# Loads and transposes at the head of the last stage: wo by one transfer a chunk, a gated tile loaded before the products end, and a gated tile's transposes moved behind the attention products

## The chip, the cores and the metric

The kernel runs on one core of one Trainium2 chip. The metric is the device time of one execution in microseconds (us), as the median of several runs. Beside it the hardware profiler recorded one execution, whose rows are shown below. TensorE is written PE (matmuls, transposes) and PEld (its weight loads), VectorE is DVE, ScalarE is ACT, GpSimd is POOL, and SP is SyncE, which issues most of the transfers; SPq is SP's queue of issues.

## The reference

x is 2048 tokens by 512, all in float32. The result is x plus two mixers of the layer-normed x:

```python
xn = layernorm(x)
# A: 32 heads of 16, feature map phi(t) = [softmax(t @ w_phi), softmax(-t @ w_phi)] per head
num = phi(q) @ (phi(k)^T @ v);  den = phi(q) . sum(phi(k)) + 1e-6
A = (num / den) @ wo                              # wo 512 x 512
# B: gated MLP with a product over the tokens
z1, z2 = halves of gelu(xn @ w_in)                # 688 columns each
g = w_sp @ layernorm(z2) + b_sp                   # w_sp 2048 x 2048
B = (z1 * g) @ w_out                              # w_out 688 x 512
out = x + A + B
```

## The kernel before

Tokens go in 16 tiles of 128. Every large product is made of three TensorE passes over operands that are split in a high and a low part (`mm3`, lines L51, L52, L53; the high part is rounded by ACT at L43, `round_h`, and the low part is the rest, made by DVE at L47, `rest_l`). The stages follow each other: projections of q, k, v with the features, the two halves of the gated MLP's input, the product with w_sp (seven products of half the size in both directions, in 32 steps; the loop's steps are numbered n, NC is their count), and a last stage. What each stage needs later goes through arrays in device memory: `e_d` holds the exponentials of the q features, `u_d` the gated tiles, `kvT_d` the summed phi(k)^T v.

The last stage takes token tiles in pairs. For tiles i and i+1 a round consists of:

- `attend_T`: 16 TensorE transposes of the features into `ptq` (L749 where the tile is plain float32, L751 otherwise), and four ACT copies into `f` (L753);
- `attend`: 32 small products `po` of `f` and `kvT` (L765), then two ACT and two DVE instructions that split the result into `oT`;
- `gated`/`gate_T` for each tile: four transposes into `ptu` (L640), two more in a second `ptu` (L644, L645), then ACT and DVE split them into `uh`, `ul` and `rt` (L43, L47, L648);
- `project_u` for each tile: 17 matmuls into `pout` by the split w_out (`wu`; 15 of `mm3` and two at L779);
- `project_o` for each tile: 12 matmuls into the same `pout`, by the split wo (`wo_h`, `wo_l`, named `woh` and `wol` in the profile), then a DVE add of x (L788) and the store (L789).

The gated tile `u` for token tile i comes by `load_u` (L634) from `u_d`. Tile 0 is loaded and transposed during the products (`first_gate`, its tile is named `u_uh`); tile 1 is loaded by `fetch_u`, whose memory, a pool called `cw`, takes the space that the products' operands leave. `slot()` gives buffers of another pool, 16 wide, freed earlier. wo is loaded in four chunks of 128 rows: `load_w` takes for every chunk four pieces of 32 rows, each piece 64 rows from the next in wo, and lays them under each other in a tile `wof`; then `round_h` and `rest_l` split it.

The order of instructions on each engine is set by a tile scheduler, which places an instruction by its own estimate; `tc.issue_after(x)` only holds the scheduler from placing an instruction ahead of x. `lasts` keeps the last instruction of some steps for that: `lasts[2]` the last transpose of a gated tile, `lasts[3]` the last `po` product. SP issues its transfers in its own order, and the eight completion semaphores of SP's queue go round: an issue waits until the transfer eight places earlier on SP has landed.

Of the kernel before, what the change touches and what calls it, by code (L numbers as in the profile page):

```python
# [10 lines left out]
F32 = mybir.dt.float32  # L11
F32R = mybir.dt.float32r
# [6 lines left out]
P = 128  # L19
S, D, H, DH, FH = 2048, 512, 32, 16, 688  # L20
# [3 lines left out]
NG = 4  # L24
NF = 2 * D
KF = FH // P
REM = FH - KF * P
# [4 lines left out]
HP, QP = P // 2, P // 4  # L32
# [3 lines left out]
def mixer(ctx: ExitStack, tc: tile.TileContext, x, x_t, wv, wqkT, phi_bd, wo, w_in, wst, b_r, w_out, out):  # L36
    nc = tc.nc
    pe, act, dve, pool, sp = nc.tensor, nc.scalar, nc.vector, nc.gpsimd, nc.sync


    def round_h(eng, h, src):
        if eng is act:
            return act.activation(h, src, AF.Copy).ins  # L43
        return eng.tensor_copy(h, src).ins

    def rest_l(l, src, h, eng=None):
        return (eng or dve).tensor_tensor(l, src, h.bitcast(F32), op=ALU.subtract).ins  # L47
# [113 lines left out]
    with ExitStack() as p0:  # L161
# [32 lines left out]
        def fold(wT, g, accs):  # L194
            gs = slice(g * P, (g + 1) * P)
            for c, acc in accs:
                ins = pe.matmul(acc[:, gs], wT[g][:, c * P:(c + 1) * P], bd[:, gs], start=g == 0, stop=g == NG - 1,
                                skip_group_check=True).ins
            return ins
# [26 lines left out]
        def split_x(src):  # L226
            t = xz.tile([P, 2, FH], F32R, tag="xz", name="xT")
            xT.append(t)
            src = src.rearrange("p a b -> p (a b)")
            return round_h(act, t[:, 0, :D], src), rest_l(t[:, 1, :D], src, t[:, 0, :D])  # L230

        def stats(s):
            st6 = wk.tile([P, 6], F32, tag="st6", name="st6")
            dve.bn_stats(st6, xt[s])
            nm = wk.tile([P, 1], F32, tag="nm", name="nm")
            ins = dve.bn_aggr(mv_x[:, s], st6).ins
            pool.tensor_scalar_mul(nm, mv_x[:, s, 0:1], -1.0)
            rstd_of(mv_x[:, s], r_x[:, s:s + 1])
            return nm, ins
# [4 lines left out]
        def transposed(s):  # L244
            xs = xt.pop(s)
            pt = ps.tile([P, ND, P], F32, tag="mm", name="pt")
            for c in range(ND):
                ins = pe.transpose(pt[:, c], xs[:, c * P:(c + 1) * P], ident).ins  # L248
            return pt, ins
# [46 lines left out]
        with ExitStack() as queue:  # L296
# [3 lines left out]
            nm, i = stats(0)  # L300
            keep(dve=i, act=center(0, nm))
            accs = [(c, (za, kv_ps_p)[c // 2].tile([P, D], F32, tag="z", name="fold")) for c in range(ND)]
            for g in range(NG):
                if g == NG - 1:
                    pt, i = transposed(0)
                    keep(pe=i)
                keep(pe=fold(wkT, g, accs))
            i, j = split_x(pt)
            keep(act=i, dve=j)
            nm, i = stats(1)  # L310
# [10 lines left out]
            pt, i = transposed(1)  # L321
            keep(pe=i)
            i, j = split_x(pt)
            keep(act=i, dve=j)
            nm, i = stats(2)
# [3 lines left out]
            for k in range(2):  # L329
                accs = [(2 * k + m, za.tile([P, D], F32, tag="z", name="fold")) for m in range(2)]  # L330
                for g in range(NG):
                    i = fold(wqT, g, accs)
                folded(0, accs)
                if k == 0:
                    keep(pe=i)
                    pt, i = transposed(2)
# [63 lines left out]
    def load_a(n):  # L400
        i, q = SEQ[n]
        f = []
        for k in range(2):
            t = ws.tile([P, QC, P], F32, tag=f"f{k}", bufs=2, name="wf")
            sp.dma_start(t, wst[2 * i + k, :, q * QC:(q + 1) * QC, :])
            f.append(t.rearrange("p (k two) t -> p two k t", two=2))
        return f
# [128 lines left out]
    for s in range(NT):  # L536
# [13 lines left out]
        r = zw.tile([P, 1], F32, tag="rstd", bufs=2, name="rstd")  # L550
# [24 lines left out]
    def load_z1(i):  # L575
        t = gt.tile([P, 2, FH + REM], F32, tag="z1", name="z1t")
        for k in range(2):
            pool.dma_start(t[:, k, :FH], z1_d[2 * i + k])
        return t

    def products(n, g):
        i, q = SEQ[n]
        ops = A.pop(n)
        for name, an, bn in FORM:
            if n % NQ == 0:
                g[name] = psg.tile([P, D], F32, tag="g", name="g")
            dst = g[name][:, :FC]
            for k in range(2):
                (ah, al), (bh, bl) = ops[an], B[2 * q + k][bn]
                mm3(dst, (ah[:, k], al[:, k]), (bh, bl), n % NQ == 0 and k == 0, n % NQ == NQ - 1 and k == 1)  # L590
# [16 lines left out]
    def gate(i, cb, z):  # L607
        cb, first, _ = cb
        with tc.issue_after(first):
            act.activation(z[:, :, :FH], z[:, :, :FH], AF.Gelu_apprx_tanh)  # L610
        zs = z[:, :, :FH].rearrange("p k (j f) -> p k j f", j=2)
        dve.tensor_tensor(zs, zs, cb.rearrange("p (k j) f -> p k j f", k=2), op=ALU.mult)
        rm = slice(KF * P, FH)
        rh = gt.tile([P, 2, REM], F32R, tag="rh", name="rh")
        dve.tensor_copy(rh, z[:, :, rm])
        rest_l(z[:, :, FH:FH + REM], z[:, :, rm], rh)
        dve.tensor_copy(z[:, :, rm], rh.bitcast(F32))
        for k in range(2):
            pool.dma_start(u_d[2 * i + k], z[:, k])
# [3 lines left out]
    def slot(name, dt=F32):  # L623
        return xz.tile([P, 2, FH], dt, tag="xz", name=name).rearrange("p a b -> p (a b)")

    def load_w(src, parts, h, l, t):
        rows = 0
        for r0, r1 in parts:
            sp.dma_start(t[rows:rows + r1 - r0], src[r0:r1, :])
            rows += r1 - r0  # L630
        return round_h(act, h, t[:rows]), rest_l(l, t[:rows], h)

    def load_u(i, t):
        sp.dma_start(t.bitcast(F32), u_d[i])  # L634
        return t
# [23 lines left out]
    lasts, wu = [None] * 5, []  # L659

    def first_q(s):
        e = slot("eq", F32R)[:, :NF]
        sp.dma_start(e.bitcast(F32), e_d[s, :, :NF])
        return e
# [11 lines left out]
    g, es, ets = {}, {}, {}  # L676
    for n in range(NC):
        i = SEQ[n][0]
        if n % NQ == 1 and i < NP - 1:
            z = load_z1(i)  # L680
        products(n, g)
        if n % NQ == NQ - 1 and i < NP - 1:
            gate(i, drain(i, g, gt.tile([P, 4, FC], F32, tag="c", name="c")), z)
            g = {}
        if n + 3 < NC:
            raw[n + 3] = load_a(n + 3)
        if n + 2 < NC:
            A[n + 2] = prep_a(n + 2, raw.pop(n + 2))
        if n == NC - 4:
            stage_w()  # L690
        if n == NC - 3:
            zs = slot("zb", F32R)
            zb, ident_r = zs[:, :NF].bitcast(F32), zs[:, NF:NF + P]
            round_h(act, ident_r, ident)
            sp.dma_start(zb, zb_d)
            uT = [first_gate(0)]
            ets[2] = load_q(2, slot("et"))
            es[2], last = q_fin(ets.pop(2), slot("qtmp")[:, :NF], zb)
        if n == NC - 2:
            es[0], es[1] = first_q(0), first_q(1)  # L700
            ets[3] = load_q(3, slot("et"))
    cb = drain(NP - 1, g, slot("c").rearrange("p (a b) -> p a b", a=4))
# [4 lines left out]
    gt = p2.enter_context(right("gl", 1))  # L707
    cw = ctx.enter_context(left("cw", 1))
    wk = ctx.enter_context(left("cwk", 2))
    us, fin = {}, []  # L710

    def fetch_u(i):
        return load_u(i, cw.tile([P, FH + REM], F32R, tag="u", bufs=4, name="u"))
# [11 lines left out]
    def gated(z, ps=None):  # L725
        return gate_T(*(ps or (pst, "tr")), z, wk.tile([P, KF, P], F32R, tag="uh", name="uh"),
                      wk.tile([P, KF, P], F32R, tag="ul", name="ul"), wk.tile([2 * REM, P], F32R, tag="rt", name="rt"))

    us[1] = fetch_u(1)
    kvT = cw.tile([P, 2 * NG, QP], F32, name="kvT")  # L730
    with tc.issue_after(cb[1]), tc.issue_after(cb[2]):
        uT.append(gated(us.pop(1), (psg, "g")))
# [60 lines left out]
    wo_h, wo_l = (cw.tile([P, ND, D], F32R, name=f"wo{k}") for k in "hl")  # L793
    p = {0: project_u(0, uT.pop(0))}
    with tc.issue_after(lasts[0]), tc.issue_after(lasts[1]), tc.issue_after(fin[-1]):
        for c in range(ND):
            rows = [(r, r + QP) for r in range((c % 2 * NG * 2 + c // 2) * QP, D, 2 * QP)][:NG]
            load_w(wo, rows, wo_h[:, c], wo_l[:, c], cw.tile([P, D], F32, tag="wof", bufs=4, name="wof"))
    fT = attend_T(0)
    p[1] = project_u(1, uT.pop(0))  # L800
    oT, ins = attend(fT)
# [13 lines left out]
    nxt = {}  # L815
    for i in range(0, NT, 2):
        if i:
            p[i] = project_u(i, nxt.pop(i))
            if i + 2 < NT:
                nxt[i + 2] = gated(us.pop(i + 2))  # L820
            with tc.issue_after(lasts[2]):
                oT, _ = attend(fT)
            with tc.issue_after(lasts[3]):
                p[i + 1] = project_u(i + 1, nxt.pop(i + 1))
        else:
            nxt[2] = gated(us.pop(2))
        if i + 3 < NT:
            nxt[i + 3] = gated(us.pop(i + 3))
        for k in range(2):
            project_o(i + k, oT, p.pop(i + k))  # L830
            ahead(i + k)
        if i == GATE_LAST:
            with tc.issue_after(lasts[0]), tc.issue_after(lasts[1]):
                gate(NP - 1, cb, z)
            p2.close()
        if i + 2 < NT:
            with tc.issue_after(lasts[4]):
                fT = attend_T(i + 2)
# [33 lines left out]
```

## Time and profile before

| | |
|---|---|
| median of 3 runs | 649.38 us (649.12 to 649.71) |
| profiled execution | 649.57 us, of which the recorded span is 647.8 us |
| TensorE clock granted | 1.000 in the mean |
| PE busy | 638.2 us (99% of the span), 4291 instructions |
| DVE, ACT, POOL busy | 509.5 us, 278.7 us, 96.3 us |
| DMA | 39077 packets, 98.12 MB, mean 151 GB/s |

A row of the timeline reads: start in us, duration in us, engine, line, operation, out<-in, shapes, count of equal instructions that follow each other; in brackets the time the engine was idle before and what ended it. Matmuls are pipelined, so a row's duration is longer than the distance to the next start. In the table of waits a row is: engine, tile and line that waited, what it waited for, total us, times, longest.

### The profile page before, as it was taken

What the parts mean: (1) busy time and instruction counts of PE and PEld (TensorE: products, weight loads), DVE (VectorE), ACT (ScalarE), POOL (GpSimd) and SP (SyncE); (2) the same over time, 40 slices, a digit from 0 to 9 for tenths busy, and PEclk for the clock granted to TensorE, in tenths of its full rate; (3) what the DMA queues carried; (4) which work ended last, traced back from release to release, by engine and by line L of the source; (5) the groups of instructions that cost most, each with busy time, mean ns of one, the idle gap of its engine ahead of it and who ended that gap; (6) DMA issues with size and microseconds to landing.
All of it is one profiled execution on the core that took longest, in us unless ns stands there. A gap on an engine that the chain in (4) does not pass through costs nothing.

```text
span 647.8 us, 11206 instructions
## 1 busy us (share of the span) xinstructions
PE 638.2 (99%) x4291; PEld 576.1 (89%) x4291; DVE 509.5 (79%) x922; ACT 278.7 (43%) x464; POOL 96.3 (15%) x185
## 2 busy tenths in 40 slices
PE   7999999999999999999999999999999899999997
PEld 6888888888888999999999999999999677888885
DVE  4988888898889579889978778678696498989521
ACT  5644344332333437887443434434353332323330
POOL 3332221101100104542010010110100000001000
PEclk9999999999999999999999999999999999999999
DMA  8265345533463951002453352544548677775620
GB/s 308 76 165 129 110 119 121 155 114 102 125 183 98 291 187 66 2 2 65 142 179 124 122 175 79 172 128 120 178 157 277 201 271 261 243 264 222 225 66 32
DMA packets 39077, 98.12 MB, mean 151 GB/s; under 512 B 4880, under 2 KB 7184, under 8 KB 39024
## 3 DMA queue, kind: packets, MB, share of 16 engines
q1 hardware_dynamic: 27824, 56.51, 27.4%
q0 software_dynamic: 8896, 35.26, 18.0%
q10 hardware_dynamic: 2304, 5.64, 2.3%
q8 instruction: 33, 0.54, 0.3%
q14 instruction: 20, 0.16, 0.1%
HBM read 56.24 MB, written 26.48 MB: 128 GB/s over the span
## 4 chain that ended last, share of the span: by engine, by line
PE 95%; DMA 2%; DVE 1%; SPq 1%; ACT 0%; issue 0%; POOL 0%; ACTq 0%; POOLq 0%
PE g L53 11%; PE g L52 11%; PE g L51 11%; PE proj L53 7%; PE proj L51 7%; PE proj L52 7%; PE zps L53 6%; PE zps L52 6%; PE zps L51 6%; PE pout L51 5%; PE pout L53 5%; PE pout L52 5%; PE po L765 2%; PE kvps L273 1%; PE ptq L751 1%; PE pt L248 1%
## 5 line engine op out<-in xcount | busy, mean ns | idle before, releaser
L53 PE MATMUL g<-B,A 128*128 128x344 f32 x448 | 143.3, 320 | 0.0
L52 PE MATMUL g<-B,A 128*128 128x344 f32 x448 | 143.2, 320 | 0.0
L51 PE MATMUL g<-B,A 128*128 128x344 f32 x448 | 143.2, 320 | 0.0
L53 PEld LDWEIGHTS g<-B,A 128*128 128x128 f32 x448 | 84.2, 188 | 0.0
L51 PEld LDWEIGHTS g<-B,A 128*128 128x128 f32 x448 | 84.2, 188 | 0.0
L52 PEld LDWEIGHTS g<-B,A 128*128 128x128 f32 x448 | 84.1, 188 | 0.0
L47 DVE TENSOR_TENSOR A<-S,A 128x512 fp32r<-128x512 f32 x64 | 43.8, 690 | 33.6 <-ACT A L43 32.7
L43 ACT ACTIVATE A<-S 128x512 fp32r<-128x512 f32 x64 | 40.1, 631 | 58.9 <-PE g L53 36.0
L110 ACT ACTIVATE e<-e,r_x 128x1024 f32<-128x1024 f32 x32 | 36.8, 1151 | 41.2 <-DVE e L109 40.4
L51 PE MATMUL proj<-wqk_h,xT 128*128 128x512 f32 x128 | 51.4, 401 | 0.3 <-ACT wqk_h L43 0.3
L52 PE MATMUL proj<-wqk_l,xT 128*128 128x512 f32 x128 | 50.5, 394 | 1.1 <-DVE wqk_l L47 1.1
L43 ACT ACTIVATE A<-wf 128x512 fp32r<-128x512 f32 x64 | 33.4, 522 | 40.6 <-PE g L53 39.7
L53 PE MATMUL proj<-wqk_h,xT 128*128 128x512 f32 x128 | 50.9, 397 | 0.0
L51 PE MATMUL zps<-w_0h,xT 128*128 128x344 f32 x128 | 41.8, 326 | 0.0
L112 DVE TENSOR_REDUCE sm<-e 128x64 f32<-128x1024 f32 x32 | 38.7, 1208 | 3.3 <-ACT e L110 3.3
L51 PE MATMUL zps<-w_1h,xT 128*128 128x344 f32 x128 | 41.0, 320 | 0.0
L53 PE MATMUL zps<-w_0h,xT 128*128 128x344 f32 x128 | 41.0, 321 | 0.0
L53 PE MATMUL zps<-w_1h,xT 128*128 128x344 f32 x128 | 41.0, 320 | 0.0
L52 PE MATMUL zps<-w_0l,xT 128*128 128x344 f32 x128 | 40.9, 320 | 0.0
L52 PE MATMUL zps<-w_1l,xT 128*128 128x344 f32 x128 | 40.9, 319 | 0.0
L47 DVE TENSOR_TENSOR A<-wf,A 128x512 fp32r<-128x512 f32 x64 | 35.5, 555 | 3.4 <-ACT A L43 3.0
L753 ACT ACTIVATE f<-ptq 128x512 f32<-128x512 f32 x32 | 16.5, 602 | 33.6 <-PE ptq L751 27.1
(194 smaller groups left out, 1429.2 us busy)
## 6 DMA issues: line engine op xcount, KB each, us to landing
wf<-in_wst SPq DMA_DIRECT2D x64, 256.0 KB, 3.3
e_d<-e POOLq DMA_DIRECT2D x16, 544.0 KB, 5.0
et<-e_d SPq DMA_DIRECT2D x16, 544.0 KB, 5.2
zacc<-e POOLq DMA_DIRECT2D x16, 512.0 KB, 5.3
er<-et POOLq DMA_DIRECT2D x12, 512.0 KB, 4.1
u_d<-z1t POOLq DMA_DIRECT2D x16, 368.0 KB, 4.1
u<-u_d SPq DMA_DIRECT2D x15, 368.0 KB, 4.6
z_d<-z1f ACTq DMA_DIRECT2D x16, 344.0 KB, 3.4
```

The source lines that it names most:

```text
L43: return act.activation(h, src, AF.Copy).ins
L47: return (eng or dve).tensor_tensor(l, src, h.bitcast(F32), op=ALU.subtract).ins
L51: pe.matmul(dst, ah, bh, start=start, stop=False)
L52: pe.matmul(dst, ah, bl, start=False, stop=False)
L53: return pe.matmul(dst, al, bh, start=False, stop=stop).ins
L110: act.activation(e, e, AF.Exp, scale=scale)
L112: dve.tensor_reduce(sm, heads(e), axis=AX.X, op=ALU.add)
L248: ins = pe.transpose(pt[:, c], xs[:, c * P:(c + 1) * P], ident).ins
L273: pe.matmul(kv_acc[k:k + QP, m // 4], vs[:, m * QP:(m + 1) * QP], e[:, m * HP:(m + 1) * HP], start=s == 0 and m < 4, stop=s == NT - 1, ski ...
L751: pe.transpose(pt[:, a, k].bitcast(F32R), src, ident_r)
L753: act.activation(f, pt.rearrange("p a k b -> p a (k b)"), AF.Copy)
L765: lasts[3] = pe.matmul(po[r][c * QP:(c + 1) * QP, j // NG], kvT[rows, j], fs[j // 2][rows, j % 2], start=True, stop=True).ins
```

## The change

Three edits.

1. The second gated tile (`us[1]`) is loaded two steps before the products end (n == NC - 2), ahead of the loads of tile 0's and 1's features (`eq`), into a buffer of the 16-wide pool that nothing uses any more (`slot("u1", F32R)`; its tile reads `u_5390` in the listing of the changed program). Before, it was loaded by `fetch_u(1)` behind those loads, into `cw`.
2. Each chunk of wo is loaded by one transfer: the four pieces of 32 rows become the first dimension of the source pattern, [4 pieces, 32 rows, 512], and the destination is the whole tile of 128 partitions. Four transfers of 256 KB stand where sixteen of 64 KB stood.
3. In the loop of rounds, the gating of tile i+3 is held back until the last `po` product (`lasts[3]`).

```diff
@@ during the products @@
         if n == NC - 2:
+            us = {1: load_u(1, slot("u1", F32R)[:, :FH + REM])}
             es[0], es[1] = first_q(0), first_q(1)
             ets[3] = load_q(3, slot("et"))
...
-    us, fin = {}, []
+    fin = []
...
-    us[1] = fetch_u(1)
     kvT = cw.tile([P, 2 * NG, QP], F32, name="kvT")
@@ the loads of wo @@
         for c in range(ND):
-            rows = [(r, r + QP) for r in range((c % 2 * NG * 2 + c // 2) * QP, D, 2 * QP)][:NG]
-            load_w(wo, rows, wo_h[:, c], wo_l[:, c], cw.tile([P, D], F32, tag="wof", bufs=4, name="wof"))
+            t = cw.tile([P, D], F32, tag="wof", bufs=4, name="wof")
+            sp.dma_start(t, wo.rearrange("(a g b j) d -> a b g j d", a=2, g=NG, b=2)[c % 2, c // 2])
+            round_h(act, wo_h[:, c], t)
+            rest_l(wo_l[:, c], t, wo_h[:, c])
@@ the rounds @@
         if i + 3 < NT:
-            nxt[i + 3] = gated(us.pop(i + 3))
+            with tc.issue_after(lasts[3]):
+                nxt[i + 3] = gated(us.pop(i + 3))
```

On SP, around the end of the products, the issues before stood as follows (`u_uh` and the first `u` are the gated tiles 0 and 1, `et` and `eq` feature loads, `wof` the loads of wo; in brackets the semaphores waited for: DMAHW those that go round, DMASW those of GpSimd's transfers, PE, DVE and Pool those of the engines):

```order
L634 DMA u_uh<-u_d 128x736 [waits DMAHW4_49,DMASW2_49,PE_49]
L373 DMA et<-e_d 128x1088 [waits DMAHW5_49,DMASW0_49,PE_49]
L663 DMA eq<-e_d 128x1024 [waits DMAHW6_49,PE_49]
L663 DMA eq<-e_d 128x1024 [waits DMAHW7_49,PE_49]
L373 DMA et<-e_d 128x1088 [waits DMAHW0_49,PE_49]
L634 DMA u<-u_d 128x736 [waits DMASW5_49,DMASW3_49,DMAHW1_49,PE_49,Pool_49]
L735 DMA kvT<-kvT_d 128x256 [waits DMAHW2_49,PE_49]
L629 DMA wof<-in_wo 32x512 [waits DMAHW3_49]
L629 DMA wof<-in_wo 32x512 [waits DMAHW4_49]
```

Now they stand so:

```order
L373 DMA et<-e_d 128x1088 [waits DMAHW5_49,DMASW0_49,PE_49]
L634 DMA u_5390<-u_d 128x736 [waits DMAHW6_49,DMASW3_49,PE_49]
L663 DMA eq<-e_d 128x1024 [waits DMAHW7_49,PE_49]
L663 DMA eq<-e_d 128x1024 [waits DMAHW0_49,PE_49]
L373 DMA et<-e_d 128x1088 [waits DMAHW1_49,PE_49]
L735 DMA kvT<-kvT_d 128x256 [waits DMAHW2_49,PE_49,Pool_49]
L798 DMA wof<-in_wo 128x1x512 [waits DMAHW3_49,PE_49]
L798 DMA wof<-in_wo 128x1x512 [waits DMAHW4_49,PE_49]
L798 DMA wof<-in_wo 128x1x512 [waits DMAHW5_49]
L798 DMA wof<-in_wo 128x1x512 [waits DMAHW6_49]
L634 DMA u<-u_d 128x736 [waits DMAHW7_49,DMASW6_49]
```

The load of gated tile 1 moved ahead of three feature loads, `kvT` took the memory and the wait that this load had, and the sixteen pieces of wo became four transfers, the first two of which wait for a matmul of the products.

On PE, the round of tiles 2 and 3 (the round of 4 and 5 alike) had this order before:

```order
L749 MATMUL ptq<-ident,et 128x128 x12
L640 MATMUL ptu<-zb,u 128x128 x4
L644 MATMUL ptu_5760<-zb,u 128x128
L645 MATMUL ptu_5760<-zb,u 96x128
L765 MATMUL po<-f,kvT 32x256 x12
L640 MATMUL ptu<-zb,u 128x128 x4
L765 MATMUL po<-f,kvT 32x256 x4
L51 MATMUL pout<-wu,uh 128x512
```

The second group of `ptu` is gated tile i+3; its last two transposes stood behind the 17 matmuls of `project_u`. In the changed program the same place reads (a `po` product counts once here and twice in the profile):

```order
L749 MATMUL ptq<-ident,et 128x128 x12
L640 MATMUL ptu<-zb,u 128x128 x4
L644 MATMUL ptu_5748<-zb,u 128x128
L645 MATMUL ptu_5748<-zb,u 96x128
L765 MATMUL po<-f,kvT 32x256 x16
L51 MATMUL pout<-wu,uh 128x512
```

and behind `project_u` stand all six transposes of the tile:

```order
L779 MATMUL pout<-wu,rt 128x512 x2
L640 MATMUL ptu<-zb,u 128x128 x4
L644 MATMUL ptu_5806<-zb,u 128x128
L645 MATMUL ptu_5806<-zb,u 96x128
L51 MATMUL pout<-woh,oT 128x512
```

So the `po` products run in one group and the four transposes moved behind `project_u`. From the round of tiles 6 and 7 on, PE's order is the same in both programs.

## The prediction

> **What bounds the kernel now.** I read the page's totals first, then the table of waits of PE in the last stage, then the chain that ended last, then the timeline at each place that the edits touch. The page says that PE is the bound everywhere:
>
> ```profile
> span 647.8 us, 11206 instructions
> PE 638.2 (99%) x4291; PEld 576.1 (89%) x4291; DVE 509.5 (79%) x922; ACT 278.7 (43%) x464; POOL 96.3 (15%) x185
> ```
>
> So an edit pays only where PE stands idle or runs worse than it can. From 480 us on, PE's table of waits has two entries:
>
> ```profile
> PE ptu L640 <- DMA u<-u_d: 1.3, 1, 1.3
> PE po L765 <- ACT f L753: 0.7, 1, 0.7
> ```
>
> The first is the end of the products. In the timeline, the last product starts at 503.08 and the transposes of gated tile 1 at 504.75; the load that they need was issued at 497.65 and is listed with 7.0 us to landing in the DMA view of 496 to 504:
>
> ```profile
> 497.65 0.32 SPq L634 DMA_DIRECT2D u<-u_d  x1
> 502.96 0.32 SPq L735 DMA_DIRECT2D kvT<-kvT_d  x1
> 502.92 0.32 PE L52 MATMUL g<-B,A 128*128 128x344 f32 x1
> 503.08 0.32 PE L53 MATMUL g<-B,A 128*128 128x344 f32 x1
> 504.75 0.52 PE L640 MATMUL ptu<-zb,u 128*128 128x128 f32 x4 [1.35 <-DMA u<-u_d]
> ```
>
> The second belongs to the loads of wo. The chain shows sixteen issues one behind the other (0.42 us each), the landing of the last piece, then ACT's `f`, which stands on ACT behind the four `woh` copies, then `po`:
>
> ```profile
> 509.84 0.77 SPq L629
> 510.65 3.52 DMA wof<-in_wo
> 514.87 0.59 ACT f L753
> 515.50 2.10 PE po L765 x32
> ```
>
> The last piece landed at 510.65 + 3.52 = 514.17, and `po` began 1.33 us later. It also took 2.10 us, for it keeps pace with `f`. The timeline of ACT and PE:
>
> ```profile
> 514.33 0.63 ACT L43 ACTIVATE woh<-wof 128x512 fp32r<-128x512 f32 x1 [3.25 <-DMA wof<-in_wo]
> 514.87 2.04 ACT L753 ACTIVATE f<-ptq 128x512 f32<-128x512 f32 x4
> 508.79 0.62 PE L779 MATMUL pout<-wu,ul_rt 96*128 96x512 f32 x2
> 509.26 1.49 PE L751 MATMUL ptq<-zb,eq 128*128 128x128 f32 x16
> 514.14 0.62 PE L779 MATMUL pout<-wu,rt 96*128 96x512 f32 x2
> 565.92 1.09 PE L765 MATMUL po<-f,kvT 64*32 64x256 f32 x32
> 566.95 0.50 PE L51 MATMUL pout<-wu,uh 128*128 128x512 f32 x1
> ```
>
> Where `f` is ready, the 32 `po` take 566.95 - 565.92 = 1.03.
>
> The rows of SP's queue and of the DMA views that the first two edits need (columns of an issue: KB of one, median us to landing; the last two rows are those of 505 to 515 us):
>
> ```profile
> 490.59 3.63 SPq L663 DMA_DIRECT2D eq<-e_d  x2
> 503.33 7.75 SPq L629 DMA_DIRECT2D wof<-in_wo  x16
> 511.17 0.84 SPq L634 DMA_DIRECT2D u<-u_d  x2
> wof<-in_wo SPq DMA_DIRECT2D x16, 64.0 KB, 1.9
> 9.00:12.00 3.00, 1.58 (x12) 1.08 (x10) 2.14 (x5) 2.79 (x6) 0.42 (x2) 1.00 1.05 398
> q1 hardware_dynamic: 27824, 56.51, 27.4%
> u<-u_d SPq DMA_DIRECT2D x4, 368.0 KB, 4.6
> xr<-in_x SPq DMA_DIRECT2D x3, 256.0 KB, 5.4
> ```
>
> **Edit 1, gated tile 1 early.** Its issue moves from 497.65 to where the first `eq` issue stood, 490.59. It then has over 12 us for a transfer that took 7.0, so PE goes from the last product to the transposes at product spacing: 503.08 - 502.92 = 0.16, start at 503.24 instead of 504.75, 1.51 us. What it is moved past: the two `eq` and one `et` loads come up to 3.3 us later, but `eq` is read only by `ptq` (from 509.26 - 1.51 = 507.75 then), and the gap of 5.3 us between SP's issues at 497.65 and 502.96 takes up the shift. On ACT and DVE a copy and a split of the last product group's drain each change places with a neighbour; I price that at nothing, because the transposes (0.52 us in the row above) run before PE needs a drained buffer, and what might remain falls into the wait at `po` below. Edit 1's gain stands only as long as nothing else stops PE before `po`.
>
> **Edit 2, wo.** The 16 issues of 7.75 us become four. `kvT` takes the memory and the wait of the old load of gated tile 1, so it can issue at about 497.65, and the first wo transfer waits, in the built program, for the product that stands 15 places before the last: 503.08 - 15 x 0.156 + 0.32 = 501.1 us; the second waits for a product six places later, about 502.0, and the others follow at about 0.5 us each, all out by 503.1. How long 1 MB then takes is not in the trace, because every transfer in it has 32 or more entries in its outermost dimension, and the new one has 4 (pieces of 32 rows). Two bounds. If it spreads over all 16 engines as the old ones did, the rate in the streaming stage applies, the windows row 9 to 12 (mean DMA share 1.05, 398 GB/s): 1.05 MB in 2.6 us, plus the fixed part of a transfer, 1.9 - 0.16 = 1.7 us (median landing of a 64 KB piece, less its bytes at that rate): last landing at or before about 506. If the outermost dimension deals the work out, each of the four pieces goes to one engine and 4 of 16 carry the lot: 398 / 16 x 4 = 99.5 GB/s, 10.5 us, last landing 501.1 + 1.7 + 10.5 = 513.3; by the average of the page's queue row, 56.51 MB / (0.274 x 16 x 647.8 us) = 19.9 GB/s an engine, 13.2 us and a landing at 516.0. I take four engines, since a transfer has to be cut into shares somewhere and its slowest dimension is the cut that keeps each piece of 64 KB whole; and of the two rates one near streaming, because between 505 and 515 us only these loads, x and gated tiles are listed: landing at 513.8.
>
> The Trainium skill, "DMA: Bandwidth & Descriptors", in the section "Why a DMA increments its semaphore by 16 and not by 1", says that the number of engines is the largest number up to 16 that divides both patterns' slowest dimension, which here (4 and 128) is 4; its "Rules for kernel authors" warn that an outermost dimension below 16 confines a transfer to that many engines. By it the sum is mine; read the other way, all 16, it is that of the first rival. No row of before has such a transfer, so the trace neither agrees nor disagrees.
>
> What follows for PE. After edit 1, PE reaches `po` at 514.14 + 0.47 - 1.51 = 513.10 (0.47 is the distance from an L779 pair to the next start, 508.79 to 509.26). With landing at 513.8, `f` still stands behind the `woh` copies and `po` starts 1.33 later, at 515.13, with the same 2.10: 0.37 us earlier than before. So edits 1 and 2 together give 0.37; edit 1's 1.51 turns into a longer wait of PE for `f` (513.10 to 515.13, about 2.0 instead of 0.7). With landings of 513.3 and 516.0 it is +0.87 and -1.83. The two gated tiles behind wo on SP (u of 2 and 3, issued at 511.17 before) are issued about 7 us earlier, queue behind wo on the four engines for 736 KB / 398 GB/s = 1.9 us and are wanted after `po`, 3.4 us behind the last landing: covered. Sixteen issues fewer also let the x loads go earlier, on which nobody waits.
>
> **Edit 3, the rounds of 2/3 and 4/5.** Rows of PE in the timeline, first of the rounds of 2 and 4, then of 6:
>
> ```profile
> 530.44 1.07 PE L765 MATMUL po<-f,kvT 64*32 64x256 f32 x24
> 531.43 0.54 PE L640 MATMUL ptu<-zb,u 128*128 128x128 f32 x4
> 531.90 0.64 PE L765 MATMUL po<-f,kvT 64*32 64x256 f32 x8
> 532.47 0.50 PE L51 MATMUL pout<-wu,uh 128*128 128x512 f32 x1
> 536.53 0.23 PE L644 MATMUL ptu<-zb,u 128*128 128x128 f32 x1
> 536.65 0.45 PE L51 MATMUL pout<-woh,oT 128*128 128x512 f32 x1
> 548.30 1.07 PE L765 MATMUL po<-f,kvT 64*32 64x256 f32 x24
> 550.33 0.50 PE L51 MATMUL pout<-wu,uh 128*128 128x512 f32 x1
> 571.00 0.46 PE L640 MATMUL ptu<-zb,u 128*128 128x128 f32 x4
> 571.46 0.47 PE L51 MATMUL pout<-woh,oT 128*128 128x512 f32 x1
> 529.02 2.06 ACT L753 ACTIVATE f<-ptq 128x512 f32<-128x512 f32 x4 [6.41 <-PE ptq L749]
> 582.87 1.09 PE L765 MATMUL po<-f,kvT 64*32 64x256 f32 x32
> ```
>
> From the first `po` to `pout` takes 532.47 - 530.44 = 2.03 in the round of 2 and 550.33 - 548.30 = 2.03 in that of 4, with four transposes in the middle; the undivided group of round 6 takes 1.03. Splitting the group costs more than the four transposes themselves. They are now paid behind `project_u`: there round 6 has 571.46 - 571.00 = 0.46 for all six, the round of 2 had 536.65 - 536.53 = 0.12 for two, so 0.34 is added. Net 2.03 - 1.03 - 0.34 = 0.66 a round. Against it, the fourth `f` ends at 529.02 + 2.06 = 531.08 and `po` would want it at about 531.1: I take off 0.02, 0.64 a round, 1.28 for both. From above it is bounded by the whole rounds: `po` to `po` is 17.86 and 17.62 in the two rounds and 582.87 - 565.92 = 16.95 in round 6, 0.91 + 0.67 = 1.58; from below by nothing, should DVE or ACT, whose work on that tile now comes later, make the `pout` behind it wait. Round 6 in that order shows no such wait (PE's table above has none), so I stay at 1.28.
>
> **The sum.** The profiled execution took 649.57. 649.57 - 0.37 - 1.28 = 647.92. It stands 0.19 above the median of the runs, so the median should be about 647.7.
>
> **Rivals.**
> - wo lands in time after all, on 16 engines (about 506). Then PE goes straight into `po` at 513.10 with `f` long ready (ptq ends by 509.3, four copies of 0.5), takes 1.03 and ends at 514.13 instead of 517.60: 3.47 with edit 1, 4.75 with edit 3, 644.6 in the median. For it speaks that all loads so far ran at the full rate; against it the four entries.
> - Slower: the four engines run below the average rate, because all four transfers are dealt to the same few engines, which would have to serve the loads of x and of gated tiles in between. It decides from a last landing of 516.75 on (516.75 + 1.33 - 515.50 = 2.58, less 1.28 is 1.30, the 0.2% of this kernel that a measurement can tell from no change): 516.75 - 502.8 = 13.95 us for 1.05 MB, 18.8 GB/s an engine, just below the average. At 15 us (517.8) it is 3.63 - 1.28 = 2.35 slower, about 651.7. Against it: those loads are issued behind wo.
> - The average rate of 19.9 GB/s, landing 516.0: 1.83 lost, 1.28 won, 649.9, no change.
> - Edit 3 does nothing, since what is saved at `po` is waited for at the next `pout`: 649.57 - 0.37 - 0.19 = 649.0, no change. The rounds' own spacing speaks against it.
>
> **How the numbers follow.** Four engines near the streaming rate 0.58, at 647.7 and within 646.6 (landing 513.0, rounds 1.58) and 649.0 (landing 515.1); all 16 engines 0.15; the average rate 0.12; slower 0.07; edit 3 at nothing 0.08. Faster by over 0.2% is below 648.1: the 0.15 and most of the 0.58 (landings up to 514.1), together 0.65; slower 0.07; the rest, 0.28, within. The range takes in the 16 engines at its lower end, with up to 0.3 more from the rounds, and half of the average-rate case at the upper: 644.3 to 649.4, with about 0.8.
>
> **What would show it.** Right: `ptu` directly behind the last product at about 503.2; four wo issues between 501 and 503.2, their landings 2.6 us apart up to 513 or 514; a wait of PE for `f` of about 2.0 us, ended by `woh` and the wo transfer behind it; the two rounds of 17.2 and 17.0. Wrong: a wo landing by 506 and no wait at `po` (the first rival), or one past 516, and `po` to `pout` above 1.1 in the round of 2.

## The result, and the profile after

The changed kernel took 654.84 us (653.75 to 655.20, four runs) against 649.55 us (649.12 to 650.59) for the kernel before in the same runs: a ratio of 1.0078, 95% interval 1.0065 to 1.0090. It is slower by 5.3 us where 1.7 us less were forecast. The profiled execution took 653.75 us with a span of 652.0 us, 4.2 us longer than the span before. It is the fastest of the four; what follows accounts for its 4.2 us, and not for the further 1.1 us between the two medians.

PE's table of waits from 480 us on, which had two entries before, has one:

```profile
PE po L765 <- ACT f L753: 6.2, 1, 6.2
```

The wait for gated tile 1 is gone, as the first edit should make it; the wait for `f` grew from 0.7 to 6.2 us. The timeline shows both places. The last product begins at 503.25 and the transposes follow at product spacing (0.15 instead of 1.67 us):

```profile
503.25 0.32 PE L53 MATMUL g<-B,A 128*128 128x344 f32 x1
503.40 0.46 PE L640 MATMUL ptu<-zb,u 128*128 128x128 f32 x4
512.73 0.62 PE L779 MATMUL pout<-wu,rt 96*128 96x512 f32 x2
519.57 2.54 PE L765 MATMUL po<-f,kvT 64*32 64x256 f32 x32 [6.22 <-ACT f L753]
```

PE reaches `po` at 513.2 (512.73 + 0.47), nearly as forecast (513.10), and stands there until 519.57 instead of the forecast 515.13. The reason is on ACT, whose `f` stands behind four copies of wo, each of which waits for its transfer:

```profile
506.80 0.62 ACT L43 ACTIVATE woh<-wof 128x512 fp32r<-128x512 f32 x1
510.76 0.63 ACT L43 ACTIVATE woh<-wof 128x512 fp32r<-128x512 f32 x1 [3.34 <-DMA wof<-in_wo]
515.22 0.63 ACT L43 ACTIVATE woh<-wof 128x512 fp32r<-128x512 f32 x1 [3.82 <-DMA wof<-in_wo]
518.40 0.63 ACT L43 ACTIVATE woh<-wof 128x512 fp32r<-128x512 f32 x1 [2.56 <-DMA wof<-in_wo]
518.94 2.04 ACT L753 ACTIVATE f<-ptq 128x512 f32<-128x512 f32 x4
```

The chain that ended last says the same in one piece of 15 us:

```profile
502.78 0.53 SPq L798
503.36 15.02 DMA wof<-in_wo
518.94 0.59 ACT f L753
519.57 2.54 PE po L765 x32
```

SP's queue shows that the issues were not late (the four wo transfers went out from 501.24 on, where 501.1 was forecast, and gated tiles 2 and 3 from 504.02 instead of 511.17):

```profile
490.76 0.32 SPq L634 DMA_DIRECT2D u<-u_d  x1
497.81 0.32 SPq L735 DMA_DIRECT2D kvT<-kvT_d  x1
501.24 2.67 SPq L798 DMA_DIRECT2D wof<-in_wo  x4
504.02 2.52 SPq L634 DMA_DIRECT2D u<-u_d  x2
```

How many engines carried wo can be read off in two ways. The first is the table by windows; its last three columns are PE's granted clock, the mean busy share of the 16 DMA engines, and GB/s:

```profile
503.50:506.50 3.00, 3.00 (x19) 2.52 (x18) 3.00 (x7) 0.77 (x2) 0.00 (x0) 1.00 0.25 94
508.00:515.00 7.00, 5.34 (x34) 4.25 (x32) 0.84 (x2) 0.63 (x1) 0.00 (x0) 1.00 1.04 245
518.50:522.50 4.00, 2.93 (x36) 1.25 (x36) 0.69 (x1) 2.82 (x6) 0.00 (x0) 0.50 0.26 101
```

With wo alone (first row) a quarter of the engines is busy and 94 GB/s move: four engines. The second way is the times, in the trace's record of semaphores, at which a transfer's completion semaphore was raised, in us, for the first wo transfer and for gated tile 2 behind it:

```
wo, chunk 0:    502.36 | 506.48 506.56 506.75 506.77
gated tile 2:   508.96 ... 510.00 (12 of them) | 518.76 518.77 519.08 519.25
```

The wo transfer has one event at its start and one from each of four engines. The gated tile, cut over 16, was done on twelve engines at 510.0 and on the other four only when wo was through, 9 us later. That agrees with what the Trainium skill says in "DMA: Bandwidth & Descriptors" ("Why a DMA increments its semaphore by 16 and not by 1"): four engines by the slowest dimension, and the sequencer raises the semaphore by the remaining 12 at once.

The accounts of the two traces against each other, first `po` of each round:

| first po of the round | before | after | later by | change in it |
|---|---|---|---|---|
| 0 | 515.50 | 519.57 | 4.07 | +4.07 |
| 2 | 530.44 | 535.28 | 4.84 | +0.77 |
| 4 | 548.30 | 552.74 | 4.44 | -0.40 |
| 6 | 565.92 | 569.98 | 4.05 | -0.39 |
| 8 | 582.87 | 586.92 | 4.05 | 0.00 |

So there are three amounts to explain: the wait at the first `po`, 0.77 us behind it, and 0.39 to 0.40 us for each of the two rounds of the third edit, where 0.64 was forecast.

### The profile page after: what moved, and what is told of

Same layout as the page of the kernel before. It is cut to its first block, busy times and chain, and to the rows that moved or that the text cites. A ratio compares the mean times of both kernels' runs of the same rounds, so it can differ in the third digit from the quotient of the medians.

```text
span 652.0 us, 11181 instructions
## 1 busy us (share of the span) xinstructions
PE 638.4 (98%) x4291; PEld 577.5 (89%) x4291; DVE 508.6 (78%) x922; ACT 278.5 (43%) x464; POOL 97.6 (15%) x185
## 4 chain that ended last, share of the span: by engine, by line
PE 95%; DMA 3%; DVE 0%; ACT 0%; issue 0%; POOL 0%; SPq 0%; ACTq 0%; POOLq 0%
PE g L53 11%; PE g L52 11%; PE g L51 11%; PE proj L53 7%; PE proj L51 7%; PE proj L52 7%; PE zps L53 6%; PE zps L52 6%; PE zps L51 6%; PE pout L51 5%; PE pout L52 5%; PE pout L53 5%; DMA wof<-in_wo 2%; PE po L765 2%; PE kvps L273 1%; PE ptq L751 1%
## 5 line engine op out<-in xcount | busy, mean ns | idle before, releaser
L51 PE MATMUL pout<-wu,uh 128*128 128x512 f32 x75 | 30.8, 410 | 0.0
```

The lines of the kernel that those rows point to most:

```text
L51: pe.matmul(dst, ah, bh, start=start, stop=False)
```

## Experiments

Theory A: wo's transfers run on four engines, which the loads beside them slow further, and TensorE's clock drops in the wait. Rivals: a transfer of 256 KB at this place, or SP's new order, is late whatever the pattern (B); a source in pieces with a step is slow as such (C). Every ratio is to the kernel before, in runs on the same chip.

**wo in one plain piece.** The rows of wo are put into the chunks' order before the launch.

```diff
-            sp.dma_start(t, wo.rearrange("(a g b j) d -> a b g j d", a=2, g=NG, b=2)[c % 2, c // 2])
+            sp.dma_start(t, wo[c * P:(c + 1) * P, :])
...
-        "wo": f(A_wo),
+        "wo": f(f(A_wo).reshape(2, NG, 2, QP, D).transpose(2, 0, 1, 3, 4).reshape(D, D)),
```

> The changed kernel with wo's rows laid out in the order of the chunks before the launch, so that each of the four transfers reads 128 rows in a row (outermost dimension 128 in place of 4); every engine's instruction order is that of the changed kernel. Theory A (the wo transfers of the change run on four of the 16 DMA engines, are slowed there by loads that run beside them, and PE's clock drops in the long wait): the last wo piece lands by about 506, PE does not wait at po, and with edit 1 (1.5 us), the wait and pace at po (0.7 + 1.0) and the two rounds (0.4 each) the time is about 645.5, 4 us below the kernel before. Theory B (a wo transfer of 256 KB with its wait on the products, or the order of SP's queue after edit 1, is what is late, whatever the pattern): last landing stays at 515 to 518, time 653 to 655.

Measured: 646.13 us, ratio 0.9941 (0.9926 to 0.9955). ACT's copies run without a stop and PE enters `po` with no wait:

```profile
506.94 2.18 ACT L43 ACTIVATE woh<-wof 128x512 fp32r<-128x512 f32 x4
509.02 2.03 ACT L753 ACTIVATE f<-ptq 128x512 f32<-128x512 f32 x4
512.86 0.62 PE L779 MATMUL pout<-wu,rt 96*128 96x512 f32 x2
513.41 1.09 PE L765 MATMUL po<-f,kvT 64*32 64x256 f32 x32
```

Same instructions in the same order on every engine, same bytes, same place on SP: only the pattern differs, and with it 8.7 us. Theory B falls. The last of wo landed at 507.7, later than the 506 expected and still before PE needed `f`. This version beats both kernels.

**wo in 16 pieces again** (edits 1 and 3 without 2).

> Edits 1 and 3 without edit 2: wo in 16 pieces of 32 rows. Theory A: pieces issue from about 501.2 every 0.42 us, the last at about 508, landing at about 510 to 511; ACT's f at about 512, so PE waits little or not at all at po; 645.5 to 646.5. Theory B in its form that edit 1's order of the queue is at fault: slower than the kernel before by 3 us or more.

Measured: 646.47 us, 0.9947 (0.9932 to 0.9962). The last copy of wo starts at 511.46, `f` at 512.00, and `po` at 513.64 without a wait:

```profile
511.46 0.63 ACT L43 ACTIVATE woh<-wof 128x512 fp32r<-128x512 f32 x1 [1.80 <-DMA wof<-in_wo]
512.00 2.04 ACT L753 ACTIVATE f<-ptq 128x512 f32<-128x512 f32 x4
513.64 1.09 PE L765 MATMUL po<-f,kvT 64*32 64x256 f32 x32
```

Edit 1 had already moved the sixteen pieces early enough, by letting wo start at 501.61 instead of 503.33. The second edit had nothing left to gain: even on 16 engines it is 0.3 us from this, with overlapping intervals.

**The rounds alone** (edit 3 on the kernel before).

> Edit 3 alone. The two rounds of tiles 2 and 4 were shorter by 0.40 and 0.39 us in the changed kernel, with po to pout 1.26 instead of 1.03 since the fourth f comes late. If that is edit 3's own, 648.8 (0.8 below before) with po to pout 1.26; by the prediction's price 648.3; if the shorter rounds came from something else in the changed kernel, 649.5.

Measured: 648.77 us, 0.9984 (0.9974 to 0.9994). Rounds from 529.61 to 547.08 to 564.30: 17.47 and 17.22, 0.40 less each than before (17.86 and 17.62, to rounding), and `po` to `pout` 1.27:

```profile
529.61 1.34 PE L765 MATMUL po<-f,kvT 64*32 64x256 f32 x32
530.88 0.50 PE L51 MATMUL pout<-wu,uh 128*128 128x512 f32 x1
```

**wo's pattern alone** (edit 2 on the kernel before).

> Edit 2 alone. Theory A: the four transfers go out from about 503.3 to 505.5, two us later than in the changed kernel, so the last lands at about 520 and po starts at about 521.3 in place of 515.5; with PE's lower clock after the stop 0.8 us more: 649.5 + 5.8 + 0.8 = about 656. Theory B, edit 1's order at fault: within 1 us of the kernel before.

Measured: 658.26 us, 1.0125 (1.0105 to 1.0145), 2.3 us more than the 656 expected; the wait is

```profile
PE po L765 <- ACT f L753: 8.0, 1, 8.0
```

and `po` started at 522.56, 1.3 later than expected. From it to the next round's `po` it is 16.80 us instead of the 14.94 before, 1.9 more where 0.8 was expected; in it the granted clock stayed at 0.50 until 528.6 (the last section has the row). So the edits add up, within the intervals (about 1 us for each ratio): edit 2 costs 8.5 us by itself and 654.84 - 646.47 = 8.4 beside the others, edit 3 gains 1.0 (0.8 in its trace), and edit 1, which was not run alone, gains 648.77 - 646.47 = 2.3 beside edit 3.

**Other cuts of the same transfer.** Only the pieces differ: 16 of 8 rows, 8 of 16, 2 of 64. The rows of wo so arrive in another order than the products need: what these three kernels compute is not the reference, but the work and its sizes are the same.

```diff
-            sp.dma_start(t, wo.rearrange("(a g b j) d -> a b g j d", a=2, g=NG, b=2)[c % 2, c // 2])
+            sp.dma_start(t, wo.rearrange("(g b j) d -> b g j d", g=16, b=ND)[c])
```

> The changed kernel with another cut of wo: each chunk's transfer reads 16 pieces of 8 rows, 32 rows apart ([16, 8, 512] in place of [4, 32, 512]); the rows so come in another order than the products need, which leaves the work and its timing the same. Theory A (the outermost dimension deals a transfer out to the engines): 16 engines, last landing by about 506, no wait at po, about 645.5. Theory C (a source in pieces with a step between them is slow as such): landing at 515 or later, 653 or more.

> As before with 8 pieces of 16 rows ([8, 16, 512], row order again another). Theory A: eight engines, about 200 GB/s, 5.3 us for the four: last landing at about 508.5 (later if the gated tiles' loads slow it, up to 511), f in time or nearly so, 645.5 to 646.5. Theory C: 653 or more.

> As before with 2 pieces of 64 rows ([2, 64, 512], row order again another). Theory A: two engines, 50 GB/s, 21 us alone, more with the loads beside them at the measured 16.4 GB/s an engine, 32 us: last landing between 524 and 535, po 1.3 us later, time between 660 and 671. Theory C: as the changed kernel, 653 to 655.

| pieces (outermost dimension) | starts of ACT's four wo copies | time, us | ratio (95%) |
|---|---|---|---|
| 16 | 506.89, then without a stop | 645.77 | 0.9944 (0.9927 to 0.9961) |
| 8 | 506.63, the next without a stop, 509.17, 511.61 | 646.78 | 0.9971 (0.9947 to 0.9995) |
| 4 (the change) | 506.80, 510.76, 515.22, 518.40 | 654.84 | 1.0078 (1.0065 to 1.0090) |
| 2 | 511.14, 516.35, 522.67, 528.92 | 665.02 | 1.0239 (1.0214 to 1.0264) |

A source with a step is as fast as a plain one when it has 16 pieces, so theory C falls; below 16, fewer pieces mean later landings. The three new rows rest on three, four and two runs. Two pieces came within the expectation; with eight the last landing (511.6) and the time lie a little beyond its upper ends (511 and 646.5); with sixteen the time came out as expected, although wo landed at 508.4 instead of 506. With two pieces, while wo was alone, the share of the engines was two sixteenths:

```profile
507.00:511.00 4.00, 4.00 (x29) 3.43 (x28) 1.13 (x2) 0.27 (x1) 0.00 (x0) 1.00 0.13 50
```

**The loads beside wo held back.** A one-column write on DVE behind the last wo chunk's split, into the tiles that are loaded next, holds those loads on SP.

```diff
+    def hold(t, ins):
+        with tc.issue_after(ins):
+            dve.memset(t, 0.0)
...
+        if after is not None:
+            hold(t.bitcast(F32)[:, :1], after)
+        return load_u(i, t)
...
-        us[s] = fetch_u(s)
+        us[s] = fetch_u(s, held)
```

> The changed kernel with the loads of the gated tiles 2 to 5 and of x held on SP until the last wo chunk is split (one-column writes on DVE into their tiles stand behind that split; the loads overwrite them). Theory A with company (loads on the 16 engines beside wo lengthen its packets from 84 to about 150 ns): wo alone streams at 84 ns a packet of 2 KB, 10.5 us, last landing at about 513.3 in place of 518.4, po at 514.6, PE's clock stays up; the held loads are then late by one to two us at the gated tile's transposes: 648.5 to 650.5. Theory A without company (four engines are simply slower than 25 GB/s each): last landing stays at about 518, and the held loads land at 522: 658 or more.

Measured: 654.11 us, 1.0072 (1.0050 to 1.0094), neither of the two expectations, since it tested half of what was meant: two gated tiles that were not held went ahead on SP. But the copies of wo show where they ran beside it: 507.55, 511.25, 513.86 and 516.48, the second 3.70 us behind the first (with the tiles' loads), the others 2.61 and 2.62 (without). The second form holds all of them:

> The run before held only two of the four gated tiles' loads: the loads of tiles 4 and 5 went ahead on SP, ran beside wo from 507 to 511, and only behind them did wo's packets return to 84 ns. Here the loads of gated tiles 2 to 5 and three of x are all held until the last wo chunk is split. Theory A with company: every wo packet of 2 KB takes about 84 ns from 505 on, pieces land 2.6 us apart, the last at about 515 (first piece at 507.2 and three times 2.6), po at about 516.2; then the held loads make PE wait some 1 to 3 us at the transposes: 650 to 654 as a time, the landing is what tells. Theory A without company: pieces 3 to 4 us apart, last at 518 or later.

```profile
506.91 0.63 ACT L43 ACTIVATE woh<-wof 128x512 fp32r<-128x512 f32 x1
509.51 0.63 ACT L43 ACTIVATE woh<-wof 128x512 fp32r<-128x512 f32 x1 [1.97 <-DMA wof<-in_wo]
512.12 0.63 ACT L43 ACTIVATE woh<-wof 128x512 fp32r<-128x512 f32 x1 [1.98 <-DMA wof<-in_wo]
514.72 0.63 ACT L43 ACTIVATE woh<-wof 128x512 fp32r<-128x512 f32 x1 [1.96 <-DMA wof<-in_wo]
505.00:513.00 8.00, 8.00 (x46) 6.59 (x44) 3.11 (x6) 2.17 (x4) 0.00 (x0) 1.00 0.27 103
```

The pieces come 2.60 us apart, which is 262144 bytes at 100 GB/s, the forecast's streaming rate; the last copy starts at 514.72, 3.7 us earlier than in the changed kernel, and `po` at 515.89. The time is 652.90 us, 1.0059 (1.0045 to 1.0073), because the held loads then make PE wait: from this `po` to the next round's it is 18.34 us instead of 14.94. In it PE waited 1.4 and 0.3 us ahead of the transposes of gated tiles 2 and 3, and the granted clock stood at 0.50 from 521.35 to 524.76. (The table of waits puts the 1.4 down to DVE's `oT`; but the load of tile 2 landed at 519.22, and PE's wait ended at 519.24.)

**PE kept at work in the wait.**

```diff
+        for k in range(warm):
+            last = pe.transpose(po[0][:, k % 2, :P], ident, ident).ins
+        if warm:
+            ctx.enter_context(tc.issue_after(last))
...
-    oT, ins = attend(fT)
+    oT, ins = attend(fT, 56)
```

> The changed kernel with 56 transposes of the identity (about 0.1 us each at full clock, about 5.7 us in all) on PE behind the second project_u, into the po buffer that is overwritten after: they fill most of the wait for f. If the wait cost more than its length because TensorE's granted clock fell to 0.50 in it, then the clock stays at 1.00, po to the next po falls from 15.7 to 14.9 us and the time by 0.8, to about 654.0. If the 0.77 came from something else (the late loads), the time stays at 654.8 or above.

Measured: 653.32 us, 1.0060 (1.0048 to 1.0072), 1.5 us below the changed kernel. In the trace wo is as late as before, but the clock stays up and `po` takes 2.10 instead of 2.54:

```profile
513.41 6.28 PE L762 MATMUL po<-ident 128*128 128x128 f32 x56
520.06 2.10 PE L769 MATMUL po<-f,kvT 64*32 64x256 f32 x32 [0.37 <-ACT f L753]
521.00:523.00 2.00, 2.00 (x31) 1.23 (x27) 0.16 (x1) 1.26 (x3) 0.00 (x0) 1.00 0.26 100
```

From this `po` to the next round's it is 534.99 - 520.06 = 14.93, the 14.94 of the kernel before; the changed kernel had 15.71. So the 0.77 us were the clock. The two profiled executions differ by only 0.3 us (653.44 against 653.75): the 0.77, less the 0.49 by which `po` begins later here. The rest of the 1.5 lies between the changed kernel's profiled execution and its median, and is not explained.

## Why the prediction was wrong

- **Edit 1: right.** 503.40 for the transposes (503.24 forecast) and 513.2 for reaching `po` (513.10). It gains 2.3 us where wo is not in the way (wo in pieces, edit 3 in both); in those two traces 1.1 of it is an earlier `po` (513.64 against 514.70), and 1.0 is that `po` no longer waits for each `f` (1.09 us long instead of 2.10).
- **Four engines: right.** The semaphore's events, the share of 0.25, and the row of cuts from 2 to 16 show it.
- **The rate on the four engines: the step that failed.** The prediction put wo "near streaming, because between 505 and 515 us only these loads, x and gated tiles are listed", landing at 513.8. It landed at 518.4. Two terms make the difference. The first chunk came at about 506.8 instead of 505.4 (501.1 + 1.7 + 2.6). It was issued at 501.24 and took 5.5 us; the fixed part of 1.7, read from pieces of 64 KB, was too small, and by this landing it is about 3. Why stays open: edit 1 had moved `eq`, `et` and `kvT` directly ahead of wo, and `kvT` took 6.0 us to land, where it took 2.0 before; but with edit 2 alone `kvT` took 2.0 as well, and the first chunk still 5.6 (from 503.93 to 509.57). The other three came 3.2 to 4.5 us apart, 11.6 us in all, where three times 2.60 is 7.8: 3.8 us. 1.4 + 3.8 makes 5.2, to rounding the 5.1 by which 518.4 lies behind the streaming bound of 513.3. The 3.8 comes from loads that are "issued behind wo" and so were taken for harmless. They are behind it only on the four engines; the other twelve started on them at once, and while they ran the 16 engines moved 245 GB/s at a busy share of 1.04, where the streaming stage had 398 at 1.05. Holding them back brought the 2.60 back, so these loads were the cause of the 3.8.
- **The second rival came true in its outcome, and in half of its mechanism:** the last landing (518.4) passed its turning point of 516.75, and even the average rate (516.0) was too good. All four transfers were on the same four engines, as it said; but these did not serve the other loads in between: their shares of gated tile 2 were done only at 518.76 to 519.25, behind wo. So the reason given against it, "those loads are issued behind wo", held on the four engines, and did not protect wo from what ran on the other twelve.
- **The wait's own price was left out.** The prediction let PE lose the time in which it stood. In 516 to 517 us the granted clock fell, stayed at 0.50 until about 523.1, and made `po` and what followed 0.77 us longer:

```profile
516.00:517.00 1.00, 0.00 (x0) 0.00 (x0) 0.57 (x1) 0.00 (x0) 0.00 (x0) 0.64 0.84 243
522.00:523.00 1.00, 1.00 (x12) 0.96 (x8) 0.21 (x1) 0.84 (x2) 0.00 (x0) 0.50 0.27 93
523.00:524.00 1.00, 1.00 (x10) 0.91 (x9) 1.00 (x3) 1.00 (x4) 0.00 (x0) 0.95 0.12 40
```

- **Edit 3: right in kind, 0.40 instead of 0.64 a round.** The term that was too small is the late fourth `f`, put at 0.02. In both rounds `po` to `pout` takes 1.26 where round 6 takes 1.03, so it is 0.23:

```profile
535.28 1.33 PE L765 MATMUL po<-f,kvT 64*32 64x256 f32 x32
536.54 0.50 PE L51 MATMUL pout<-wu,uh 128*128 128x512 f32 x1
```

In the trace, four of the third eight `po` start at 535.95, 0.03 behind the end of the fourth `f` (533.86 + 2.06 = 535.92). The kernel before paid for the late `f` as well: its 24 `po` ahead of the transposes took 0.99 (530.44 to 531.43), where three quarters of 1.03 are 0.77. So round 6's 1.03 was the wrong figure to subtract in these rounds; with 1.26 the sum is 2.03 - 1.26 - 0.34 = 0.43, near the 0.40.

- **The first rival's time** (644.6, all 16 engines) can be held against the plain layout's 646.13. Of the 1.5 us between them 0.48 are the rounds (2 x 0.24) and 0.4 the level of those runs (649.77 for the kernel before instead of 649.38); PE also reached `po` 0.3 later than forecast (513.41). The mechanism holds.

## What to carry to other kernels

Before several transfers are merged into one, look at the outermost dimension of the merged pattern: it, not the size, decided how many engines carried it, and a layout that makes it 16 or more cost nothing here. A transfer on few engines is not alone because later ones stand behind it in the queue; these run on the other engines at once. And a gain that comes from two edits should be asked which of them is still needed: moving one load two steps earlier had already brought the sixteen small transfers in on time.

## What the runs showed of the hardware that was not expected

Loads on 16 engines beside a transfer on four slowed everything: 245 GB/s at a busy share of 1.04 (508 to 515 us of the changed kernel). The same loads of gated tiles and x without such a transfer beside them moved 366 GB/s at 0.97 (508 to 513 us, wo in plain pieces), and the streaming stage 398 at 1.05. The packets of 2 KB (wo's and x's) took 132 ns in the median between 507 and 518, and 84 ns when wo was alone. Why was not tried: memory, the tile's partitions and the way in which packets are taken in turn are all open.

TensorE's clock was halved about 2.9 us after the last matmul of the changed kernel (its end at 513.35 and the mean of 0.64 in 516 to 517 put the step at 516.3) and came back at 523.1, about 3.5 us after work resumed at 519.57. With edit 2 alone PE stopped at about 514.6 and resumed at 522.56, and of the windows

```profile
518.00:519.00 1.00, 0.00 (x0) 0.00 (x0) 0.10 (x1) 0.63 (x1) 0.00 (x0) 0.68 0.38 110
527.00:528.00 1.00, 1.00 (x4) 0.71 (x3) 1.00 (x2) 0.55 (x2) 0.00 (x0) 0.50 0.91 198
```

the first puts the step at 518.4, 3.8 us after the stop, and the second shows the clock still halved; it came back only at 528.6, 6.0 us after work resumed. A stop of 2.6 us, with all the loads held back, did not lower it at once; there it fell at 521.35, 5.5 us after that stop had ended, behind two more waits of 1.4 and 0.3 us. By the traces' records of the granted clock, its steps lie, in every run, whole multiples of 3.41 us apart (516.27 and 523.10, 518.37 and 528.61, 521.35 and 524.76), so how long after a stop or a restart one comes varies. The Trainium skill gives about 3.4 us of idle or of busy time for the two steps ("TensorE: Matmul & The Clock Gate", "What's actually happening"); the 3.41 us between steps agrees with that figure, while the times from a stop (2.9 and 3.8 us) and from a restart (3.5 and 6.0 us) lie on both sides of it.
